# Top-k attention and a SwiGLU block: reciprocals of the first 12 units folded into the transposes on TensorE

## The chip, the cores and the metric

The kernel runs on one core of a Trainium2 chip. The metric is device time in microseconds for one launch. The engines of a core work in parallel, each through its own queue in order: TensorE (PE, with its weight loads PEld), VectorE (DVE), ScalarE (ACT), GpSimd (POOL), and SyncE (SP), which here issues nearly all DMAs. TensorE writes only into PSUM, from where ScalarE copies results into SBUF.

## The reference

Inputs q, k and v have the shape (8, 8, 576, 64): 8 batches, 8 heads, 576 positions, 64 dimensions, all fp32. The attention result becomes a matrix of 4608 rows and 512 columns, which goes through a SwiGLU block with 1536 hidden units.

```python
scores = scale * np.matmul(q, k.transpose(0, 1, 3, 2))
kth = np.partition(scores, -top_k, axis=-1)[..., -top_k:-top_k + 1]   # top_k = 32
scores = np.where(scores >= kth, scores, -1000000000.0)
scores = scores - np.max(scores, axis=-1, keepdims=True)
attn = np.exp(scores)
attn = attn / (np.sum(attn, axis=-1, keepdims=True) + 1e-09)
x = np.matmul(attn, v)            # then (B,H,S,D) -> (B*S, H*D)
g = x @ w_gate
out = (g / (1 + np.exp(-g)) * (x @ w_val)) @ w_out
```

The change concerns the division by the row sum.

## The kernel before

**Units.** The attention is cut into units: a batch, a tile of 128 query rows and a pair of heads. A batch has 576 = 4 x 128 + 64 rows, so four full query tiles and a last one of 64 rows, in which two heads share the 128 partitions. With four head pairs (`NHP` = 4) a batch has 20 units, 160 in all. The first 12 units (0 to 11) are the first three query tiles of batch 0; counted from 0, unit n is processed in iteration n of the main loop (L870), with neighbours overlapped.

**One unit, step by step.** `scores`: four products of q and k on TensorE (L325), copied and scaled by ScalarE into `sc` (L330). `select`: VectorE finds the 32 largest of each row of 576 in four rounds of MAX8 (L347) and three of MATCH_REPLACE8 (L351), for two heads. `shift`: a tiny GpSimd subtraction `bias` (L362). `weigh`: ScalarE makes the mask (L374) and the exponentials `e`, 128 x (2 x 576), with the row sums `tot` (L379), and adds the small constant (L384). `normalize`: VectorE takes the reciprocal of `tot` (L393), and for the first 12 units GpSimd multiplies each head's half of `e` by it (L399, two instructions of 128x576); from unit 12 on ScalarE does one of the two halves (L397). `turn`: TensorE transposes `e` in nine blocks of 128x128 (L412): four of head 0, one which holds the last 64 columns of head 0 and the first 64 of head 1, and four of head 1. ScalarE copies the three PSUM tiles into `et` (L413). `values`: TensorE multiplies with v (L448), ScalarE copies the result into `xT` (L465), the input of the FFN.

**The rest.** FFN work is cut into pieces that are put between the attention steps: L517 (gate and value products of the first blocks, 128 columns), L569 (first output products), L604 and L670 for all later blocks. ScalarE and GpSimd do the activation (L537 to L545, L639 to L645). The FFN weights are loaded in 36 pieces in the first 170 us and rounded by `rounded`: a DMA into a slot `w` (four slots, L109), three ScalarE instructions (L117, L119, L120), a VectorE shift (L124) and two GpSimd instructions (L125, L126). The second of these two frees the slot for the next DMA.

**Order.** The order on each engine is the order in which the program is written: at the end a dependency ties every instruction to the one before it on its engine. In iteration n the main loop issues the scores of the units ahead, `values` of units n-4 and n-3 (every second iteration), `weigh(n-1)`, the second half of the scores, the top-k of unit n with FFN pieces and weight rounding strewn in, `turn(n-2)`, then `normalize(n-1)` and `shift(n)`. So on GpSimd the bias of unit n stands behind the normalization of unit n-1. PSUM tiles of the attention come from one pool of five (`ps_t`), so `turn` also needs earlier tiles to be copied out.

Of the kernel before, what the change touches and what calls it, by code (L numbers as in the profile page):

```python
# [9 lines left out]
ALU = mybir.AluOpType  # L10
FP32 = mybir.dt.float32
# [4 lines left out]
P = 128  # L16
# [9 lines left out]
def kernel(  # L26
# [37 lines left out]
    nc = tc.nc  # L64
    B, H, S, D = q.shape
    DM, DFF = w_gate.shape
    J = S // P
    JP = J * P
    R = S - JP
    NHP = H // 2  # L70
# [4 lines left out]
    NBLK = B * S // BLK  # L75
    HALVED = 3
    AHEAD = 8 * NHP
    scale = 1.0 / float(D) ** 0.5
    assert D == 64 and R == 64 and H * D == DM and DM == 512 and B * S % BLK == 0

# [6 lines left out]
    ffn = ctx.enter_context(tc.tile_pool(name="ffn", bufs=2))  # L87
# [3 lines left out]
    ident = consts.tile([P, P], FP32, name="ident")  # L91
# [190 lines left out]
    state = {}  # L282
# [84 lines left out]
    def weigh(n):  # L367
# [10 lines left out]
        for t, hs in enumerate(heads):  # L378
# [3 lines left out]
            )  # L382
        if n < AHEAD:
            nc.scalar.add(tot[:, 0 : len(heads)], tot[:, 0 : len(heads)], EPS)  # L384
        st["tot"] = tot

    def normalize(n):
        st = state[n]
        tot, e, heads = st.pop("tot"), st["e"], st.pop("heads")
        nh = len(heads)  # L390
        for t in range(nh if n >= AHEAD else 0):
            nc.vector.tensor_scalar_add(tot[:, t : t + 1], tot[:, t : t + 1], EPS)
        nc.vector.reciprocal(tot[:, 0:nh], tot[:, 0:nh])  # L393
        yield
        for t, hs in enumerate(heads):
            if t == 0 and n >= 3 * NHP:
                nc.scalar.mul(e[:, hs], e[:, hs], tot[:, t : t + 1])  # L397
            else:
                nc.gpsimd.tensor_tensor(  # L399
                    e[:, hs], e[:, hs], tot[:, t : t + 1].to_broadcast([P, S]), ALU.mult  # L400
                )

    def turn(n):

        last = units[n][1] == J
        e = state[n].pop("e")
        et = work.tile([P, 2 * J + 1, P], FP32, tag="et", name="et")
        for c0, cn in ((0, J), (J, 1)) if last else ((0, J), (J, 1), (J + 1, J)):
            ps = ps_t.tile([P, 512], FP32, tag="t", name="etps")
            for c in range(cn):  # L410
                k0 = S - P if last and c0 == J else (c0 + c) * P
                nc.tensor.transpose(ps[:, c * P : (c + 1) * P], e[:, k0 : k0 + P], ident[:])  # L412
            nc.scalar.copy(  # L413
                et[:, c0 : c0 + cn, :],
                ps[:, 0 : cn * P].rearrange("p (c j) -> p c j", c=cn),
            )
            if c0 == J:
                yield
        state[n]["et"] = et
# [393 lines left out]
    def share(n):  # L813
# [9 lines left out]

        beside = 5.8 if n < AHEAD else 6.25
        least = 2.0 if n >= 3 * NHP and n % 2 == 0 else 0.0
# [12 lines left out]
    def pieces(n):  # L838
        for _ in range(n):
            if credit[0] >= 1:  # L840
                credit[0] -= piece()

    def run(steps):
        for _ in steps:
            pass
# [24 lines left out]
    for n in range(NU + 3):  # L870
        nh = n_heads(units[n][1]) if n < NU else 1
        topk = select(n) if n < NU else no
        norm = normalize(n - 1) if 0 <= n - 1 < NU else no
        nxt = [scores(m) for m in scored(n)]
        ahead = fetch(n + 3 if n else 2) if n + 3 < NU else no
# [42 lines left out]
        if 0 <= n - TURN < NU:  # L918
            run(turn(n - TURN))
# [6 lines left out]
        pieces(1)  # L926
        if n < AHEAD:
            run(topk)
# [55 lines left out]
```

## Time and profile before

| what | us |
|---|---|
| median of three runs | 1713.59 |
| lowest and highest | 1713.14, 1713.67 |
| the profiled execution's own time | 1712.03 |
| its span, first to last instruction | 1710.2 |
| TensorE busy in the span | 1647.4 |
| VectorE busy | 1476.5 |
| ScalarE busy | 1259.5 |
| GpSimd busy | 799.0 |

The mean granted clock of TensorE is 0.978 of full speed. A row of a timeline or of the chain of waits gives the start, the duration, the engine, and the line with the tile that it writes and those that it reads; a bracket says how long the engine was idle before it and which instruction ended that. Group rows give the number of instructions, their busy time and the mean duration of one in ns. PE instructions are pipelined, so the mean duration of one is longer than the distance from one to the next; distances are read from the chain of waits, where consecutive instructions are merged.

### The profile page before, as it was taken

Reading aid. Unit: us, or ns where it says so; the run is one execution under the profiler, and the core shown is the slowest. Engines: PE = TensorE matmul, PEld = TensorE weight load, DVE = VectorE, ACT = ScalarE, POOL = GpSimd, SP = SyncE. Lnnn points to the kernel's source line nnn. Section 1 sums busy time; section 2 is a strip of 40 time slices with the busy share of each in tenths; the row PEclk is TensorE's granted clock in tenths of the full one; section 3 lists DMA queues with packets and bytes.
Section 4 is the critical chain, followed back from the end, with each engine's and each line's share of the span. In section 5 each row is a group of like instructions: output and inputs, shape, how many; then the busy total and the mean of one; then the engine's idle time right before and its main releaser. Section 6 shows DMA issues by size and latency. Waiting matters only on the chain.

```text
span 1710.2 us, 32128 instructions
## 1 busy us (share of the span) xinstructions
PE 1647.4 (96%) x11600; PEld 1398.2 (82%) x11600; DVE 1476.5 (86%) x3311; ACT 1259.5 (74%) x2901; POOL 799.0 (47%) x914
## 2 busy tenths in 40 slices
PE   5588999999999999999999999999999999999999
PEld 3477698987888887888888888888888888888887
DVE  7999899998989899997999989998999979999400
ACT  7899887877767787768676887777777778676531
POOL 4798545352444425353535334444344433535434
PEclk6699999999999999999999999999999999999999
DMA  7533120003000030001200030000400011000000
GB/s 210 139 112 99 29 72 2 14 1 79 22 13 1 15 86 14 1 8 42 51 14 1 13 74 27 2 13 2 98 1 13 2 44 29 13 2 13 1 13 13
DMA packets 109310, 59.74 MB, mean 35 GB/s; under 512 B 88544, under 2 KB 96992, under 8 KB 109152
## 3 DMA queue, kind: packets, MB, share of 16 engines
q1 hardware_dynamic: 108016, 57.37, 12.9%
q8 instruction: 91, 1.49, 0.4%
q14 instruction: 67, 0.55, 0.1%
q10 hardware_dynamic: 1136, 0.33, 0.1%
HBM read 48.23 MB, written 9.44 MB: 34 GB/s over the span
## 4 chain that ended last, share of the span: by engine, by line
PE 88%; DVE 5%; ACT 4%; DMA 1%; POOL 1%; issue 1%; SPq 0%; POOLq 0%; ACTq 0%
PE f L604 37%; PE x_ps L670 10%; PE av L448 9%; PE s L325 8%; PE y_ps L670 8%; PE etps L412 7%; PE f L517 6%; DVE m L347 2%; DVE e L351 2%; PE kqps L271 1%; PE o_ps L569 1%; PE s L308 1%; ACT e L379 1%; DVE size L124 1%; ACT e L374 0%
## 5 line engine op out<-in xcount | busy, mean ns | idle before, releaser
L347 DVE MAX8 m<-e 128x8 f32<-128x576 f32 x864 | 617.9, 755 | 3.3
L351 DVE MATCH_REPLACE8 e<-m,e 128x576 f32<-128x576 f32 x576 | 425.4, 748 | 0.0
L604 PE MATMUL f<-xT,wg 128*128 128x256 f32 x1440 | 335.9, 382 | 1.3 <-ACT xT L465 1.3
L604 PE MATMUL f<-xT,wv 128*128 128x256 f32 x1440 | 331.4, 380 | 0.0
L604 PEld LDWEIGHTS f<-xT,wg 128*128 128x128 f32 x1440 | 268.9, 190 | 49.0 <-issue 13.1
L604 PEld LDWEIGHTS f<-xT,wv 128*128 128x128 f32 x1440 | 268.2, 190 | 37.5 <-issue 3.8
L640 POOL TENSOR_TENSOR h<-h,half_g 128x512 f32<-128x512 f32 x90 | 114.7, 1275 | 349.2 <-ACT h L639 349.2
L330 ACT ACTIVATE sc<-s 128x288 f32<-128x288 f32 x512 | 170.4, 431 | 105.2 <-PE s L325 104.6
L413 ACT COPY et<-etps 128x512 f32<-128x512 f32 (+1 forms) x448 | 183.6, 486 | 66.0 <-PE etps L412 65.6
L379 ACT ACTIVATE e<-e,bias 128x576 f32<-128x576 f32 x288 | 221.7, 780 | 12.7 <-POOL bias L362 9.7
L374 ACT ACTIVATE e<-sc,m 128x576 f32<-128x576 f32 x288 | 212.3, 792 | 0.6 <-DVE m L347 0.5
L351 DVE MATCH_REPLACE8 e<-m,sc 128x576 f32<-128x576 f32 x288 | 212.6, 748 | 0.0
L412 PE MATMUL etps<-ident,e 128*128 128x128 f32 x1312 | 178.2, 280 | 33.7 <-POOL e L399 15.0
L347 DVE MAX8 m<-sc 128x8 f32<-128x576 f32 x288 | 204.0, 747 | 7.5 <-ACT sc L330 7.5
L412 PEld LDWEIGHTS etps<-ident,e 128*128 128x128 f32 x1312 | 156.2, 144 | 54.7 <-POOL e L399 19.2
L645 POOL TENSOR_TENSOR h<-h,val 128x512 f32<-128x512 f32 x90 | 114.8, 1275 | 155.0 <-ACT val L644 152.4
L325 PE MATMUL s<-kqT 64*128 64x288 f32 x1024 | 169.2, 441 | 13.7 <-ACT sc L330 7.5
L399 POOL TENSOR_TENSOR e<-e,tot 128x576 f32<-128x576 f32 x140 | 161.1, 1154 | 28.5 <-DVE tot L393 28.2
L448 PE MATMUL av<-et,v 128*64 128x128 f32 (+1 forms) x2560 | 158.0, 268 | 0.0
L448 PEld LDWEIGHTS av<-et,v 128*64 128x64 f32 x2560 | 137.7, 140 | 5.9 <-ACT kqT L268 2.7
L325 PEld LDWEIGHTS s<-kqT 64*128 64x128 f32 x1024 | 94.2, 190 | 58.3 <-issue 18.4
L397 ACT ACTIVATE e<-e,tot 128x576 f32<-128x576 f32 x148 | 119.1, 805 | 21.7 <-DVE tot L393 21.6
(86 smaller groups left out, 2249.1 us busy)
## 6 DMA issues: line engine op xcount, KB each, us to landing
v<-in_v_dram SPq DMA_DIRECT2D x32, 256.0 KB, 3.3
kq_in<-in_k_dram SPq DMA_DIRECT2D x63, 128.0 KB, 2.8
kq_in<-in_q_dram SPq DMA_DIRECT2D x63, 128.0 KB, 2.9
w<-in_moe_w_gate_dram SPq DMA_DIRECT2D x12, 512.0 KB, 3.8
w<-in_moe_w_val_dram SPq DMA_DIRECT2D x12, 512.0 KB, 3.8
w<-in_moe_w_out_dram SPq DMA_DIRECT2D x12, 512.0 KB, 3.5
out_dram<-o SPq DMA_DIRECT2D x38, 128.0 KB, 2.4
out_dram<-o SPq DMA_DIRECT2D x16, 256.0 KB, 2.5
```

What stands on the lines that cost most here:

```text
L325: nc.tensor.matmul(ps[:, 0:half], slab[d, q0 : q0 + P], slab[d, k0 : k0 + half])
L330: nc.scalar.mul(sc[:, i * half : (i + 1) * half], ps[:, 0:half], scale)
L347: nc.vector.max(m[:, t, 8 * r : 8 * r + 8], cur[:, hs])
L351: nc.vector.match_replace(e[:, hs], m[:, t, 8 * r : 8 * r + 8], cur[:, from_[t]], LOWEST)
L374: nc.scalar.activation(e[:, hs], sc[:, at], AF.Prelu, bias=m[:, t, TOP_K - 1 : TOP_K], scale=-1.0, alpha=SMALL,)
L379: nc.scalar.activation(e[:, hs], e[:, hs], AF.Exp, bias=bias[:, t : t + 1], scale=-1.0 / SMALL, accum_out=tot[:, t : t + 1],)
L399: nc.gpsimd.tensor_tensor(e[:, hs], e[:, hs], tot[:, t : t + 1].to_broadcast([P, S]), ALU.mult)
L412: nc.tensor.transpose(ps[:, c * P : (c + 1) * P], e[:, k0 : k0 + P], ident[:])
L413: nc.scalar.copy(et[:, c0 : c0 + cn, :], ps[:, 0 : cn * P].rearrange("p (c j) -> p c j", c=cn),)
L448: nc.tensor.matmul(av[d, i, 0:ql], weights_, moving, start=c == (0 if last else J), stop=c == (J if last else J - 1),)
L604: nc.tensor.matmul(ps[:, i, :], w[:, kc, m * P : (m + 1) * P], x[:, kc, :], start=(kc == 0), stop=(kc == KC - 1),)
L670: nc.tensor.matmul(ps, lhsT, T[i][m], start=m == 0, stop=m == MQ - 1)
```

## The change

For units 0 to 11 (`SCALED = 3 * NHP`), `e` stays as the exponentials left it. GpSimd instead builds two 128x128 diagonal matrices, one for each head, with the reciprocals on the diagonal (one instruction of 128x256, from the identity matrix and `tot`). `turn` then multiplies with a diagonal matrix in place of the transpose: `e` block as the stationary operand, the diagonal matrix as the moving one, which transposes and scales at once. The block that holds columns of both heads is split into two products of 64 columns each, since its halves need different reciprocals. Four pairs of diagonal matrices are kept, in a buffer that has the tag of the FFN's output tile `o`. Units from 12 on are as before.

```diff
+    SCALED = 3 * NHP
...
+    scaling = []
+
     def normalize(n):
...
         nc.vector.reciprocal(tot[:, 0:nh], tot[:, 0:nh])
         yield
+        if n < SCALED:
+            if not scaling:
+                scaling.append(ffn.tile([P, 4, 2, P], FP32, tag="o", name="diag", bufs=1))
+            st["diag"] = diag = scaling[0][:, n % 4]
+            nc.gpsimd.tensor_tensor(
+                diag,
+                ident[:].unsqueeze(1).to_broadcast([P, 2, P]),
+                tot[:].unsqueeze(2).to_broadcast([P, 2, P]),
+                ALU.mult,
+            )
+            return
...
+        diag = state[n].pop("diag", None)
...
-                nc.tensor.transpose(ps[:, c * P : (c + 1) * P], e[:, k0 : k0 + P], ident[:])
+                at = slice(c * P, (c + 1) * P)
+                if n >= SCALED:
+                    nc.tensor.transpose(ps[:, at], e[:, k0 : k0 + P], ident[:])
+                elif c0 == J:
+                    for t in range(2):
+                        d = slice(t * R, (t + 1) * R)
+                        nc.tensor.matmul(
+                            ps[d, at],
+                            e[:, k0 + t * R : k0 + (t + 1) * R],
+                            diag[:, t],
+                            start=True,
+                            stop=True,
+                        )
+                else:
+                    nc.tensor.matmul(
+                        ps[:, at], e[:, k0 : k0 + P], diag[:, c0 // J], start=True, stop=True
+                    )
```

## The prediction

> **What bounds the kernel now.** I read the page from the top: busy shares, then the forty slices.
>
> ```profile
> PE 1647.4 (96%) x11600; PEld 1398.2 (82%) x11600; DVE 1476.5 (86%) x3311; ACT 1259.5 (74%) x2901; POOL 799.0 (47%) x914
> ...
> PE   5588999999999999999999999999999999999999
> DVE  7999899998989899997999989998999979999400
> ACT  7899887877767787768676887777777778676531
> POOL 4798545352444425353535334444344433535434
> PEclk6699999999999999999999999999999999999999
> ```
>
> From the fifth slice (171 us) on TensorE is full at full clock; before that it has gaps and a low clock. The twelve units that change lie there: the last of their GpSimd multiplications ends at 167.7 us. The same cut by stretches:
>
> ```profile
> 0.00:168.40 168.40, 117.86 (x845) 98.22 (x846) 155.61 (x323) 147.09 (x326) 127.97 (x122) 0.79 0.51 142
> 168.40:400.00 231.60, 228.02 (x1961) 194.93 (x1961) 213.67 (x464) 181.39 (x434) 111.65 (x126) 1.00 0.10 25
> ```
>
> The columns are span, then PE, PEld, DVE, ACT, POOL busy, granted clock, DMA. After 168.4 us PE lacks only 3.6 of 231.6 us, so the end moves by as much as the moment moves when PE gets there. Before it PE idles 50 us; there the question is what sets the pace. The chain of waits, asked for 100 to 180 us, answers it:
>
> ```profile
> 105.71 2.48 POOL e L399 x2
> 108.19 0.34 POOL bias L362
> ...
> 112.44 1.30 POOL wg L126
> 113.76 3.54 DMA w<-in_moe_w_out_dram
> 117.39 0.68 ACT size L117
> ...
> 132.54 0.27 ACT xT L465
> 132.94 2.15 PE etps L412 x9
> 135.10 7.04 PE f L517 x48
> ```
>
> GpSimd, with a multiplication in its queue, frees a weight slot late; the DMA behind it lands late; ScalarE then runs back to back up to the xT copy, which gives unit 8's transposes their PSUM slot. From there PE is without a gap, but for one place, in PE's timeline:
>
> ```profile
> 160.32 1.15 PE L412 MATMUL etps<-ident,e 128*128 128x128 f32 x9
> ...
> 166.65 0.66 PE L412 MATMUL etps<-ident,e 128*128 128x128 f32 x4 [1.61 <-POOL e L399]
> 167.76 0.76 PE L412 MATMUL etps<-ident,e 128*128 128x128 f32 x5 [0.45 <-POOL e L399]
> ```
>
> These are units 10 and 11; unit 11 waits 2.06 us for its two multiplications. The rows that price the operations are groups kept apart by shape:
>
> ```profile
> L412 PE MATMUL etps<-ident,e 128*128 128x128 f32 x1312 | 178.2, 280 | 33.7 <-POOL e L399 15.0 <-ACT xT L465 12.5 <-ACT e L397 3.5
> L448 PE MATMUL av<-et,v 128*64 128x128 f32 x2048 | 136.8, 277 | 0.0
> L690 POOL TENSOR_TENSOR xT<-h 128x256 f32<-128x256 f32 x51 | 36.8, 731 | 27.7 <-PE x_ps L670 25.5
> ```
>
> **What is removed on GpSimd.** Two 128x576 multiplications per unit took 2.25 to 2.48 us together (24 instructions, median 1152 ns). **Added:** one 128x256 multiplication. Its nearest row is L690's, 731 ns for 128x256; the bounds are 0.19 (bias, 128x2) and 1.15 us (128x576). I take 0.73, so GpSimd gains 1.5 to 1.75 us per unit, about 19 us in twelve. Little of it is on the path. Three places pay:
> - At 82.5 us ScalarE waits 0.73 us for the bias, queued directly behind unit 4's multiplications. The bias comes about 1.5 us earlier, so this wait goes; the xT copy behind it and the first FFN product start 0.73 earlier.
> - At 117.39 ScalarE waits 1.01 us for w_out. Two multiplications stand before that slot's release in the continuous GpSimd run from 89.8 us, so it frees some 3 us earlier and the wait goes. What is late next is ScalarE itself, without a gap to 138 us.
> - Unit 11's 2.06 us. Its diagonal matrix is still queued behind L545, L125 and L126, and starts at about 165.3, ready at 166.0.
>
> VectorE's weight shifts (L124) take 403 ns at best, 704 in the median, 1492 at most, and the long ones end when a GpSimd instruction ends; five that lie over a multiplication lose 3.5 us (excesses 0.61, 0.66, 0.60, 0.94, 0.67). I cost this at nothing: between 104 and 148 us the chain runs through GpSimd, ScalarE and PE. If ScalarE had slack, this would be the next gain.
>
> **What is added on TensorE.** Line 448 issues 1280 products with v in the program text (8 per unit, 160 units); the rows show 2048 + 512 = 2560. Line 412 issues 1312 transposes and shows 1312. So an fp32 product is two PE instructions, a transpose one. A unit goes from 9 instructions to 2 x 8 full and 2 x 2 of 64 columns. In the chain nine transposes at full clock take 0.98 us (0.109 each), 48 product instructions with 128 columns 5.36 (0.112 each), 40 of av with 64 weight columns 2.33 (0.058, two side by side). After: 16 x 0.112 + 4 x 0.058 = 2.02, and some 0.06 for two changes of array shape, so +1.1 us per unit. The bounds are +1.04 and, if the halves do not run side by side, 20 x 0.112 - 0.98 = +1.26. At half clock the nine take 2.15, the new ones 16 x 0.239 + 4 x 0.117 = 4.29: +2.14.
>
> The Trainium skill ("TensorE: Matmul & The Clock Gate", Terms) calls transpose mode four times faster for FP32. By that a unit would cost 3 x 0.98 = +2.9 us at full clock instead of +1.1, and the sum below would end some 5.4 us higher; the rows here show 0.109 against 2 x 0.112, a factor of two, and I go by them.
>
> Units 0 to 7 transpose where PE idles 2 to 5 us on either side. I cost them at nothing; the cover is PE's wait for ScalarE before each, and if a copy of et (ScalarE, in order) has to wait for the last product, it costs up to 0.9 us (unit 6: products would end at about 115.0, its third copy stood at 114.1).
>
> **The new waits.** The diagonal matrices use the buffer of the first output tile; ScalarE first writes that at 189.5 us, 20 us after unit 11. The fifth matrix waits for PE's unit 0, four units back. L124 gets a wait on GpSimd in the program, on an older piece that its ScalarE producer already awaited. All three cost nothing.
>
> **The sum on the path,** from the xT copy at 132.5 on:
> - unit 8's start: -0.73 - 1.01 = -1.74;
> - unit 8's products at half clock: +2.14;
> - the clock: it rose at 49.7, 80.4, 114.6, 121.4 and 138.5 us and fell at 118.0 and 131.7, all multiples of about 3.4 us apart, and a rise needs such a slice nearly full. If PE starts at 131.2 instead of 132.94, the slice from 131.7 is full and the rise comes 3.4 us earlier, worth 1.7 us. That hangs on a phase no one sets: -0.85, bounds 0 and -1.7;
> - units 9 and 10 in the gapless stretch: 2 x 1.1 = +2.2;
> - unit 11: +1.1 - 2.06 = -0.96. PE arrives at about 166.8, after the matrix.
>
> Together +0.79 us. The profiled execution took 1712.03 us (span 1710.2), so it would take 1712.8; the median of the three others is 1.56 above it, and on that median the forecast is 1714.4.
>
> The skill (same page, PE-mode transpose) holds that transposes do not count as activity for the clock; by it, products in their place would bring the early rise for certain, a sum of about -0.1. The rise at 49.7 followed a slice with 2.4 us of transposes in it, so the trace does not bear that out.
>
> **Rivals.**
> - *TensorE's low clock takes the gain back: slower.* Longer transposes of unit 3 fill the slice 70 to 73.5, the clock rises early, the products after it finish at 79 instead of 82, PE idles 5 us and the first FFN product at 84 starts at half clock: +1.55. Unit 6 then holds up ScalarE by 0.9. The start of unit 8 is +0.71 instead of -1.74, the clock term 0: 0.71 + 2.14 + 2.2 - 0.96 = +4.1, 1717.7 us. It decides once ScalarE loses over 1.74 us between 84 and 117. For it: PEclk 0.5 for 60 to 80 us. Against: ScalarE's copies mostly have 1 to 2 us of slack.
> - *GpSimd's relief reaches further: faster.* ScalarE also loses four waits for weights before 80 us (0.76, 0.86, 0.99, 0.84 = 3.45), and the clock rises early: -1.74 - 3.45 + 2.14 - 1.7 + 2.2 - 0.96 = -3.5, 1710.1 us. Against: those slots are freed by pieces that waited for VectorE, not for a multiplication.
> - *The products cost no more than transposes.* Then -1.74 - 0.85 - 2.06 = -4.65, 1708.9 us. The doubled record counts speak against it.
>
> **How the numbers follow.** Forecast 0.70, slower rival 0.18, far relief 0.09, cheap products 0.03. A measurement here tells 0.2% (3.4 us) from no change, so same is 1710.2 to 1717.0. Two thirds of the slower rival and a tail of the forecast lie above (0.14), two thirds of the two fast ones below, with a little of the forecast (0.08); 0.78 remains. The range from 1711.5 to 1718.0 holds the forecast with its bounds (-0.2 to +2) and most of the slower rival.
>
> **What would show it.** GpSimd's busy time before 168 us falls by about 19 us; about 240 PE instructions read the diagonal matrices, the transposing of units 9 and 10 grows from 1.0 to about 2.1 us each; no wait of unit 11 for GpSimd; L117's wait at 117 gone; PE without a gap from 131 to 134 us on. A shift of the gapless stretch beyond 3 us either way would make me wrong, above all through ScalarE's order before 117 us or through the clock.

## The result and the profile after

| | before | after |
|---|---|---|
| median, us (22 runs each; the three shown before are among them) | 1713.29 | 1715.92 |
| lowest and highest | 1711.63, 1714.59 | 1714.77, 1718.19 |
| own time of the profiled execution | 1712.03 | 1715.13 |
| its span | 1710.2 | 1713.3 |

The ratio is 1.0018, with an interval from 1.0012 to 1.0024: the changed kernel is 0.18% slower (0.15%, 2.6 us, by the medians alone; 3.1 us by the two profiled executions). The forecast was +0.8 us. The sign that it gave is right, and the time lies in its range, but three quarters of the loss were not in its sum.

Line numbers below are those of the changed kernel: L402 builds the diagonal matrices, L441 and L433 are the products that transpose (whole blocks, and blocks of 64 columns), L444 the copy of et, L496 that of xT, L548 the FFN products, L568 to L571 their activation, L118 to L121 ScalarE's part of a weight piece. L429 are the transposes and L413 the multiplications of `e` in the units that keep them, L352 is VectorE's MATCH_REPLACE8, L396 its reciprocal. In the versions with more lines they shift by two.

The page of the changed kernel, busy times and three rows of the forty slices:

```profile
PE 1664.1 (97%) x11732; PEld 1413.5 (82%) x11732; DVE 1475.0 (86%) x3311; ACT 1259.0 (73%) x2901; POOL 778.3 (45%) x902
...
PE   6698999999999999999999999999999999999999
...
POOL 4677544343444424353535334444344443535434
PEclk6699999999999999999999999999999999999999
```

TensorE has 132 instructions and 16.7 us more, GpSimd 12 instructions and 20.7 us less. From the fifth slice on TensorE is full at full clock, as it was. Up to 168.4 us, with the columns span, PE, PEld, DVE, ACT, POOL, granted clock, DMA share, GB/s:

```profile
0.00:168.40 168.40, 131.42 (x949) 110.64 (x950) 150.34 (x316) 144.36 (x322) 106.97 (x109) 0.79 0.49 139
```

GpSimd falls from 127.97 to 106.97 us here, TensorE rises from 117.86 to 131.42. The groups kept apart by shape, for the start of the changed kernel (count, then busy time and mean ns of one):

```profile
L402 POOL TENSOR_TENSOR diag<-ident,tot 128x256 f32<-128x256 f32 x12 | 7.7, 643 | 0.1
L441 PE MATMUL etps<-diag,e 128*128 128x128 f32 x192 | 37.1, 354 | 15.7 <-ACT xT L496 10.3 <-POOL diag L402 5.4
L433 PE MATMUL etps<-diag,e 128*64 128x128 f32 x48 | 6.8, 372 | 1.6 <-ACT sc L331 1.6
```

So 240 product instructions stand where 108 transposes stood. Now the order of events. TensorE's timeline around the first FFN product, before and after:

```profile
84.71 3.39 PE L517 MATMUL f<-xT,wg 128*128 128x128 f32 x28 [2.52 <-ACT xT L465]
```

```profile
78.64 0.71 PE L548 MATMUL f<-xT,wg 128*128 128x128 f32 x4
83.75 4.88 PE L548 MATMUL f<-xT,wg 128*128 128x128 f32 x28 [4.40 <-ACT xT L496]
```

and its stretches (span, PE busy, then PEld, DVE, ACT, POOL, granted clock), two of the kernel before and four of the changed one:

```profile
77.00:80.50 3.50, 3.50 (x34) 3.17 (x32) 3.50 (x9) 2.66 (x7) 3.42 (x4) 0.51 0.75 243
80.50:84.00 3.50, 1.70 (x12) 1.02 (x11) 3.50 (x10) 2.77 (x6) 2.01 (x3) 1.00 0.63 167
```

```profile
73.50:77.00 3.50, 2.99 (x42) 2.33 (x40) 3.50 (x8) 3.47 (x10) 3.42 (x3) 1.00 0.30 57
77.00:80.50 3.50, 2.35 (x22) 1.54 (x18) 3.50 (x8) 2.75 (x7) 3.42 (x4) 1.00 0.74 232
80.50:84.00 3.50, 0.25 (x1) 0.26 (x2) 3.50 (x8) 3.47 (x10) 0.22 (x2) 0.93 0.59 163
84.00:87.40 3.40, 3.40 (x19) 3.40 (x20) 3.40 (x10) 0.91 (x4) 2.66 (x2) 0.57 0.00 0
```

The clock is full from about 73 us (before: from 80.4), the products behind unit 3's transposing are over by 79.4, TensorE has nothing to do for 4.40 us, and the 28 product instructions that follow get a clock of 0.57 and take 4.88 us; before they took 3.39. ScalarE needs that result. What ScalarE waited for between 84 and 134 us (total, times, longest), before and after:

```profile
ACT h L537 <- PE f L517: 2.3, 1, 2.3
ACT size L117 <- DMA w<-in_moe_w_out_dram: 1.0, 1, 1.0
```

```profile
ACT h L568 <- PE f L548: 3.8, 1, 3.8
ACT et L444 <- PE etps L441: 1.3, 1, 1.3
```

The wait for the FFN product has grown by 1.5 us, the one for w_out is gone, and unit 6's third copy now waits for the longer products. The fall of the clock at that product is not the changed kernel's alone. Of the profiles with no filling ahead of it (the experiments below included), the three with products in the units before all show it: 4.88, 5.90 and 5.50 us for the 28 instructions, after a rise between 73 and 75 us. Of four with transposes, where the clock rose between 78.5 and 80.4 us, three took 3.36 to 3.39 us and one, of a kernel that up to there is the kernel before, 5.02. So an execution of the kernel before can pay this too, and the +1.49 us below holds for the two executions compared.

The chain of waits of the changed kernel shows both waits, and what follows:

```profile
83.43 0.27 ACT xT L496
...
83.75 4.89 PE f L548 x28
...
88.66 0.60 ACT h L568
...
111.32 2.05 PE etps L441 x8
113.37 0.63 PE etps L433 x4
113.99 2.02 PE etps L441 x8
...
133.77 2.05 PE etps L441 x8
135.82 0.62 PE etps L433 x4
136.44 1.90 PE etps L441 x8
138.34 8.93 PE f L548 x80
147.28 0.89 PE etps L441 x8
148.17 0.37 PE etps L433 x4
148.54 1.09 PE etps L441 x8
```

Where before GpSimd and a DMA stood in the chain between 104 and 117 us, there are now ScalarE and TensorE alone. Unit 8 starts at 133.77 instead of 132.94, and at half clock its twenty instructions take 4.57 us; units 9 to 11 take 2.35 us each (0.89 + 0.37 + 1.09) where 0.98 stood. Unit 11 waits for nothing.

### The profile page after: what moved, and what is told of

Same layout as the page of the kernel before. It is cut to its first block, busy times and chain, and to the rows that moved or that the text cites. A ratio compares the mean times of both kernels' runs of the same rounds, so it can differ in the third digit from the quotient of the medians.

```text
span 1713.3 us, 32373 instructions
## 1 busy us (share of the span) xinstructions
PE 1664.1 (97%) x11732; PEld 1413.5 (82%) x11732; DVE 1475.0 (86%) x3311; ACT 1259.0 (73%) x2901; POOL 778.3 (45%) x902
## 4 chain that ended last, share of the span: by engine, by line
PE 89%; ACT 5%; DVE 3%; DMA 1%; issue 1%; SPq 0%; POOL 0%; ACTq 0%; POOLq 0%
PE f L635 36%; PE x_ps L701 10%; PE av L479 9%; PE s L326 8%; PE y_ps L701 8%; PE etps L429 7%; PE f L548 7%; DVE e L352 1%; PE kqps L272 1%; DVE m L348 1%; PE o_ps L600 1%; ACT e L380 1%; PE s L309 1%; PE etps L441 1%; ACT et L444 1%
## 5 line engine op out<-in xcount | busy, mean ns | idle before, releaser
L352 DVE MATCH_REPLACE8 e<-m,e 128x576 f32<-128x576 f32 x576 | 423.8, 742 | 0.0
L444 ACT COPY et<-etps 128x512 f32<-128x512 f32 (+1 forms) x448 | 183.9, 486 | 70.3 <-PE etps L429 67.0
L352 DVE MATCH_REPLACE8 e<-m,sc 128x576 f32<-128x576 f32 x288 | 211.9, 742 | 0.0
L429 PE MATMUL etps<-ident,e 128*128 128x128 f32 x1204 | 156.3, 273 | 4.3 <-ACT e L411 3.5
L429 PEld LDWEIGHTS etps<-ident,e 128*128 128x128 f32 x1204 | 140.0, 141 | 19.7 <-ACT e L411 4.0
L413 POOL TENSOR_TENSOR e<-e,tot 128x576 f32<-128x576 f32 x116 | 133.0, 1147 | 29.7 <-DVE tot L396 29.5
```

Source lines behind the costliest of these rows:

```text
L352: nc.vector.match_replace(e[:, hs], m[:, t, 8 * r : 8 * r + 8], cur[:, from_[t]], LOWEST)
L413: nc.gpsimd.tensor_tensor(e[:, hs], e[:, hs], tot[:, t : t + 1].to_broadcast([P, S]), ALU.mult)
L429: nc.tensor.transpose(ps[:, at], e[:, k0 : k0 + P], ident[:])
L444: nc.scalar.copy(et[:, c0 : c0 + cn, :], ps[:, 0 : cn * P].rearrange("p (c j) -> p c j", c=cn),)
```

## The experiments

Two theories are held against each other. **Theory B:** TensorE's longer transposing and its low clock delay ScalarE between 84 and 117 us, and that takes GpSimd's 1.74 us of relief and more. **Theory A:** the loss is product time in TensorE's gapless stretch, from unit 8 on; TensorE's work ahead of unit 8 costs the end nothing, as the forecast had it. Unit 8's late start must then come from a gain of GpSimd's that did not reach ScalarE. Each run is compared with runs of the kernel before beside it, and each ratio below is against that.

### Products alone, and relief alone

The first kernel keeps GpSimd's multiplications of `e` and transposes by products with the identity matrix:

```diff
-        if n < SCALED:
+        if n < 0:
...
-                            diag[:, t],
+                            ident[:],
...
-                        ps[:, at], e[:, k0 : k0 + P], diag[:, c0 // J], start=True, stop=True
+                        ps[:, at], e[:, k0 : k0 + P], ident[:], start=True, stop=True
```

> Units 0 to 11 transpose by products with the identity matrix, split as in the change, and GpSimd multiplies e as before: TensorE's part of the change alone. Theory A (the loss is product time in TensorE's gapless stretch): units 9 and 10 cost 1.36 us each, unit 11 1.36 less the 2.06 us that it waited before, unit 8 some 0.8: +2.8 us against the kernel before. Theory B (the loss is TensorE's low clock, which reaches the path through ScalarE): besides these the first FFN product at 84 us runs at half clock (+1.5 us) and unit 6 holds ScalarE up by 1.3 us, of which 1.0 is absorbed by the wait for a weight slot at 117 us: +4.6 us.

Measured: 1718.21 us, ratio 1.0025 (1.0016 to 1.0034), +4.6 us. That is theory B's number, but the lower end of the interval, +2.7 us, reaches theory A's +2.8; the trace has to decide. Its chain of waits:

```profile
85.48 5.90 PE f L548 x28
...
116.25 1.99 PE etps L441 x8
118.25 0.04 DVEq L352
118.28 0.04 issue
118.32 1.55 DVE e L352 x3
...
136.33 2.05 PE etps L441 x8
```

The first FFN product is slower still (5.90 us, after 5.20 us without work on TensorE), and unit 8 starts 3.39 us later than before. On the way unit 6's products release a buffer of `e` at 118.25 for which VectorE has waited. So TensorE's part alone delays unit 8's start, by an amount that theory A has no place for. (Without filling or change ahead of unit 8, its start also moves between executions: 132.94 and, in the run with unit 11 alone below, 133.47 us. That is far less than 3.39.)

The second kernel builds the diagonal matrices but transposes with the identity matrix. It leaves out the division by the row sum in units 0 to 11.

```diff
-                if n >= SCALED:
+                if n >= 0:
```

> GpSimd builds the diagonal matrices in place of its two multiplications, and TensorE transposes with the identity as before, so the division is left out for units 0 to 11: GpSimd's part of the change alone. Both theories: unit 11's wait goes (-2.06 us). If ScalarE's two waits (0.73 and 1.01 us) go as well and are carried to unit 8, -4 us, with a clock that rises one step earlier -5.7 us. If the relief reaches no further than unit 11, -2 us.

Measured: 1707.80 us, ratio 0.9966 (0.9954 to 0.9979), -5.9 us. Its chain at unit 8:

```profile
130.51 2.18 PE etps L429 x9
132.69 5.71 PE f L548 x48
```

Unit 8 starts 2.43 us earlier than before, so GpSimd's gain does reach ScalarE, with more than the 1.74 us forecast. Theory A has no way out left. The two parts add up at that place: 3.39 - 2.43 = +0.96, against +0.83 in the changed kernel. Put the other way, TensorE's part costs 3.39 us at unit 8's start without the relief and 3.26 with it (133.77 against 130.51). The two parts don't add up at the end (4.6 - 5.9 = -1.3 against +2.6). Of that difference 2.06 us is unit 11's wait, which each of them removes: one because TensorE comes later, one because GpSimd is done earlier.

### Which units

Products in units 0 to 8 only, the three units in the gapless stretch as before:

```diff
-    SCALED = 3 * NHP
+    SCALED = 9
```

> The change for units 0 to 8 only. Theory A: without 1.36 us each for units 9 and 10, and with unit 11 back to a transpose and part of its wait, 2.7 us below the changed kernel, so about +0.4 us against the kernel before (unit 8's +1.7 less the remaining relief of unit 11). Theory B: the shift of unit 8 by +1.7 us at the end of its FFN product stays in full, and a shorter wait of unit 11 takes back at most 1 to 1.5: about +0.5 us. This run does not tell A from B, it prices units 9 to 11.

Measured: 1716.56 us, ratio 1.0014 (1.0005 to 1.0023), +2.9 us: a miss. Sparing units 9 to 11 the products brought nothing. The chain of waits:

```profile
144.38 0.60 ACT h L568
...
150.80 0.17 DVE tot L396
...
167.89 0.10 POOL e L413
...
168.81 1.15 POOL e L413
...
170.01 1.31 PE etps L429 x5
171.32 2.88 PE f L548 x16
```

The path to unit 11 does not run through TensorE here. It leaves at the FFN product behind unit 8, for which ScalarE's `h` waits (144.38, before 142.16), and goes over the reciprocal on VectorE (150.80, before 148.59) to GpSimd's multiplication (167.89, before 165.63). All of it is 2.2 us late, TensorE waits for it again, and the clock falls in that wait: 1.31 and 2.88 us for what took 0.76 and 1.79. A unit's products in the gapless stretch are a cost only where TensorE gets there last.

Unit 11 alone:

```diff
-        if n < SCALED:
+        if n == 11:
...
-                if n >= SCALED:
+                if n != 11:
```

> Only unit 11 gets its diagonal matrix and products, all others as before. Both theories: nothing moves before 165 us; unit 11 costs 1.36 us more and its wait of 2.06 us shrinks to what the matrix takes: -0.7 us against the kernel before, a version that would beat both.

Measured: 1712.68 us, ratio 0.9994 (0.9986 to 1.0003): not told from no change. The wait of 2.06 us became one of 1.11 us for the diagonal matrix, which stands behind the same weight pieces on GpSimd.

### Holding the clock up

If the half clock is the cause, work without any use in the idle stretch must give the time back. In the changed kernel 38 transposes of the identity matrix into an unused PSUM tile go ahead of the rest of the first FFN product:

```diff
+    FILL_A = 38
+    FILL_T = {}
...
+                    if (kb, t, g, i, kc) == (0, 0, 0, 0, 1) and w is wg:
+                        fill(FILL_A)
...
+    def fill(k):
+        if k:
+            idle = ps_f.tile([P, P], FP32, tag="f", name="idle")
+        for _ in range(k):
+            nc.tensor.transpose(idle[:], ident[:], ident[:])
...
+            fill(FILL_T.get(n - TURN, 0))
             run(turn(n - TURN))
```

> The changed kernel with 38 transposes of the identity into an unused PSUM tile in TensorE's gap before the rest of the first FFN product (79.4 to 83.8 us), so that its clock stays up there. Theory B (low clock through ScalarE): that product takes 3.4 us instead of 4.9, ScalarE goes on 1.5 us earlier at 88 us, and if unit 6 holds it up no more than now, unit 8 starts 1.5 us earlier: -1.5 us against the changed kernel, up to -3 with a clock that rises one step earlier at unit 8. Theory A (product time in the gapless stretch): no change.

Measured: 1713.87 us, ratio 1.0000 (0.9991 to 1.0009). Added work made the changed kernel faster, by some 2 us by the medians and 1.3 us by the profiled executions; theory A has 0. TensorE's timeline:

```profile
79.40 4.31 PE L882 MATMUL idle<-ident 128*128 128x128 f32 x38
83.99 3.39 PE L550 MATMUL f<-xT,wg 128*128 128x128 f32 x28 [0.28 <-ACT xT L498]
```

The same 28 instructions take 3.39 us, and unit 8 starts at 132.53, 1.24 us earlier than in the changed kernel.

Next the same, with 22 transposes ahead of unit 6 and 36 ahead of unit 8:

```diff
-    FILL_T = {}
+    FILL_T = {6: 22, 8: 36}
```

> As the one before, and 22 such transposes before unit 6 and 36 before unit 8, in the gaps of 2.6 and 4.3 us there. Theory B: unit 6 transposes in 2.35 us and no longer holds ScalarE up (1.33 us less), unit 8 in 2.35 instead of 4.41: together with the first product -1.5 - 1.3 - 2.1 = -4.9 us against the changed kernel, below the kernel before. Theory A: only unit 8's 2.1 us.

Measured: 1709.13 us, ratio 0.9976 (0.9966 to 0.9986): 4.4 us faster than the kernel before. Its stretches and its chain at unit 8:

```profile
80.50:84.00 3.50, 3.02 (x27) 2.78 (x26) 3.50 (x8) 3.47 (x10) 0.20 (x2) 1.00 0.48 154
84.00:87.40 3.40, 3.40 (x32) 3.40 (x32) 3.40 (x10) 1.13 (x5) 2.66 (x2) 1.00 0.02 5
```

```profile
131.00 1.13 PE etps L443 x8
132.13 0.37 PE etps L435 x4
132.50 1.09 PE etps L443 x8
133.59 8.93 PE f L550 x80
```

Unit 8 starts 2.77 us earlier than in the changed kernel and its twenty instructions take 2.59 us instead of 4.57. ScalarE has no wait for unit 6's products any more. Against the version with the first filling alone unit 8 starts 1.53 us earlier, so both of the terms that theory B names, 1.49 and 1.33 us, come back when the clock is held up.

### How much of that is the filling itself

The kernel before, with 34 transposes ahead of unit 8 only, and then with 22, 34 and 36 at the three places:

> The kernel before with 34 such transposes in the gap of 3.9 us before unit 8. There unit 8's transposes took 1.95 us instead of 0.98 at full clock and the FFN product behind them 3.42 instead of 1.79: -2.6 us against the kernel before if the clock is what costs there, 0 if PE's place in line is set by something else.

Measured: 1712.77 us, ratio 0.9996 (0.9987 to 1.0004), not the -2.6 us expected. In its profiled execution the filling did its work: from unit 8's transposes to unit 9's it is 9.91 us, against 12.59 in the kernel before. But the first FFN product had fallen to half clock (5.02 us at 84.63), and unit 8 started 1.23 us late. Unit 11 then waited as before, for a multiplication to which the chain of waits leads through VectorE and GpSimd from before 128 us on, not through unit 8. In that wait the clock fell, and the 16 FFN instructions behind it took 3.11 us instead of 1.78. The first output products start at 170.08 us, before at 170.14.

> The kernel before with transposes of the identity in its gaps before the rest of the first FFN product (22), unit 6 (34) and unit 8 (36): the clock is held up, GpSimd and the transposes are as before. If the gain of the same filling in the changed kernel came from the clock alone, it is had here as well: about -2.8 us at unit 8, and 1.5 in executions in which the first product falls to half clock; -2.8 to -4 us against the kernel before, level with the changed and filled kernel. If the relief of GpSimd is what the full clock lets through, this one gains -1 to -2 at most, as the unit 8 filling alone did, since unit 11 still waits for GpSimd and ScalarE for its weight slot.

Measured: 1710.85 us, ratio 0.9988 (0.9979 to 0.9997), -2.1 us. What TensorE waited for between 60 and 175 us, first line:

```profile
PE etps L414 <- POOL e L401: 11.5, 6, 4.4
```

In the changed kernel with fillings at the same three places, waits for GpSimd are down to one of 1.7 us, for a diagonal matrix. Even so the change adds little here. The fillings alone give 2 us of the 4.4, and the two profiled executions show where the rest lies. The first output products start at 168.26 us in this one and at 168.58 us with the change, so up to there the change has gained nothing beside the fillings. From there to the end of the span the times are 1540.0 and 1538.6 us: here the clock falls once more near the end (0.50 from 1642 to 1645 us), in the other it does not. The next section takes up that fall.

### A version that is faster than both

As the version with three fillings, but units 9 and 10 keep their transposes and GpSimd's multiplications:

```diff
-    SCALED = 3 * NHP
+    SCALED = (*range(9), 11)
...
-        if n < SCALED:
+        if n in SCALED:
...
-                if n >= SCALED:
+                if n not in SCALED:
```

> The changed kernel with the three fillings, and the change for units 0 to 8 and 11 only: units 9 and 10 in the gapless stretch are transposed and multiplied by GpSimd as before. Theory of product time: 2 x 1.36 = -2.7 us against the changed and filled kernel (about -7 against the kernel before) if GpSimd, with its work for units 9 and 10 back, has unit 11's matrix ready before TensorE arrives; if not, the wait eats up to 1.1 us of it, as in the run with unit 11 alone.

Measured: 1709.12 us, ratio 0.9979 (0.9970 to 0.9988), the same as with all twelve units, though its first output products start at 167.15 us against 168.58. Unit 11 again waits 1.13 us for its diagonal matrix, behind the multiplications of units 9 and 10. And the 1.4 us that are left went at the far end: TensorE idles 1.78 us ahead of unit 159's transposes, at 1638 to 1641 us, and in this profile the clock then fell, in that of the version with all twelve units not. From the first output products to the end it is 1540.2 us with the fall and 1538.6 without. The kernel before and the changed kernel have the same idle stretch and the same fall, with 1540.1 and 1540.0 us. From 1640 to 1647 us (span, PE busy, granted clock, DMA share, GB/s):

```profile
1640.00:1647.00 7.00, 6.92 (x61) 0.76 0.26 60
```

Whether holding the clock up there brings the difference out was tried with 15 transposes more at that place, in both versions:

```diff
-    FILL_T = {6: 22, 8: 36}
+    FILL_T = {6: 22, 8: 36, 159: 15}
```

> The changed kernel with the three fillings, and 15 identity transposes (1.64 us) ahead of unit 159's transposes, where TensorE idles 1.78 us at about 1640 us. Theory C: whether the clock falls after that idle stretch is a matter of the phase of its slices, and a fall costs about 1.5 us; the profiled execution of the version without this filling had no fall and took 1708.97, its executions lie in two groups, 1708.74 to 1709.14 (five) and 1710.35 to 1710.62 (three). Then only the lower group is left: median about 1709.0, highest under 1709.5, no half clock after 1641 us. Rival D: the two groups come from the first 170 us; then both groups stay, the filling makes no difference beyond 0.2 us.

Measured, all twelve units: 1709.05 us, ratio 0.9975 (0.9964 to 0.9985). The median stays within 0.1 us, as expected, but the upper group is not gone altogether: seven executions lie between 1708.27 and 1709.30, one at 1710.20.

> Units 0 to 8 and 11 changed, with the three fillings, and the same 15 transposes ahead of unit 159's. Theory C: the profiled execution of the version without it had half clock from 1641 to 1644.6 us and took 1709.12, with the time at which the first output products start 1.4 us earlier than in the version with all twelve units; its executions reach from 1707.31 to 1710.51. Without the fall the median is about 1707.6, 1.4 below the version with all twelve. Rival D: the median stays at 1709.1 and the spread at 3.2 us.

Measured, units 0 to 8 and 11: 1708.29 us (1707.60 to 1708.84), ratio 0.9969 (0.9958 to 0.9980). The spread falls from 3.2 to 1.2 us and the median by 0.8, not by the 1.5 expected. Its row of the same stretch:

```profile
1640.00:1647.00 7.00, 6.94 (x68) 1.00 0.25 58
```

So the fall at the end goes with most of the spread in one version and, with one execution out of eight, not all of it in the other. The gain of 0.8 us is not told from none by the ratios, whose intervals overlap. This version has the lowest median of those that keep the division, 0.31% below the kernel before. How much of that is the change and how much the four fillings stays open, since the kernel before was not run with all four. By one execution each, the first output products start at 167.12 us here and at 168.26 us in the kernel before with three fillings, a gain of 1.1 us.

## Why the prediction was right or wrong

The terms of its sum, as the two profiles have them:

| step | forecast, us | measured, us |
|---|---|---|
| bias earlier, first FFN product's start (84.71 to 83.75) | -0.73 | -0.96 |
| first FFN product at half clock | not in the sum | +1.49 |
| wait for w_out at 117 | -1.01 | -1.01 |
| unit 6's third copy of et waits | 0 (up to 0.9 named) | +1.33 |
| unit 8's start, these together | -1.74 | +0.83 |
| unit 8's products | +2.14 | +2.46 |
| clock rise, on the FFN product behind | -0.85 (0 to -1.7) | -1.63 |
| units 9 and 10 | +2.2 | +2.73 |
| unit 11 | -0.96 | -1.13 |
| sum | +0.79 | +3.26 |

TensorE's first output products start at 173.33 instead of 170.14 us (+3.19), and the span is 3.1 us longer, so the measured terms hold the whole of the difference between these two executions. Unit 8's products and the clock's rise are read from TensorE's timeline: 4.41 against 1.95 us to the start of the next product, and 1.79 against 3.42 us for that product. The clock's term came out near its bound by luck: the forecast let unit 8 start earlier, so that the clock would rise 3.4 us earlier. Unit 8 started later, and the clock rose at about 138.1 instead of 138.5 us; the longer products took up the time at half clock, and the FFN product behind them came after the rise.

**The step that failed** is "Units 0 to 7 transpose where PE idles 2 to 5 us on either side. I cost them at nothing". The cover that was named, TensorE's wait for ScalarE, hides the length of the transposing but not two things that come out of it. The longer work of unit 3 moves the clock's rise from 80.4 to about 73 us (78.5 to 80.4 in the five profiles with transposes there, 72 to 75 in the eight with products), so the work behind it ends earlier, the idle stretch grows to 4.40 us and the next product starts at a low clock; ScalarE waits for that product. And unit 6's last product, at half clock, is later than ScalarE's copy: "up to 0.9 us" was 1.33. Both were written down in the rival that ends slower, with unit 8's start at +0.71; it was +0.83. The condition that the rival set, a loss of ScalarE above 1.74 us between 84 and 117, came true: 1.49 + 1.33 = 2.82. The runs show the cause twice over. TensorE's part moves unit 8's start by 3.39 us alone and by 3.26 on top of the relief; and with the idle stretches filled unit 8 starts 2.77 us earlier than in the changed kernel, 1.24 of it from the first filling. By the medians the three fillings bring the changed kernel from 2.6 us behind the kernel before to 4.4 ahead of it. Not all of this is damage of the change undone: the kernel before gains 2.1 us by fillings too, and the fall near the end, which no filling of the three touches, makes 1.5 us between the profiled executions. A chance of 0.18 for that rival was too little, given that its chain of events was worked out and nothing stood against it but that the copies "mostly have 1 to 2 us of slack".

**The rival's own sum** of +4.1 was too high in one term and too low in others: it took the clock's rise at 0, while the longer products of unit 8 filled the slice by themselves and the FFN product behind took 1.79 us instead of 3.42.

**GpSimd's gain** was priced nearly right in busy time: the wait for w_out is gone, busy time fell by 21.0 us (forecast 19), and a diagonal matrix took 0.61 us in the median (0.73 taken, between 0.19 and 1.15). Its reach was priced low: alone it brings unit 8 forward by 2.43 us, not 1.74. The far-reaching rival, -3.5, is not what happened in the changed kernel; with the relief alone it was -5.9, of which 2.06 is unit 11's wait.

**The products** cost 2.35 us per unit at full clock, +1.37 instead of +1.1 and above the upper bound of +1.26. The halves of the split block do run side by side, as the forecast took it: in the trace the two products of a pair start 0.007 us apart, as av's do. The term that was mis-sized is the change of array shape, 0.06 us in the forecast. At full clock the first half starts 0.205 us behind the last whole block, the next whole block 0.203 us behind the last half, and the one after that 0.213 us later, where consecutive products of whole blocks are 0.112 us apart. In all it is 2.35 - 16 x 0.112 - 4 x 0.058 = 0.33 us a unit. The rival in which products cost no more than transposes fell with the first row.

**Unit 11** came out nearly as forecast. But its wait of 2.06 us belongs to a path over ScalarE, VectorE and GpSimd: in the three runs with units 9 and 10 back on GpSimd it came back, with 1.1 to 2.1 us.

**Two rules that the prediction weighed.** The products that replace nine transposes took 2.35 us against 0.98, a factor of 2.4 with the split block and its changes of shape; going by the rows was right. The Trainium skill ("TensorE: Matmul & The Clock Gate", Terms) calls transpose mode four times faster for FP32, without saying than what; against products no run here shows that. As to the clock, 38 transposes and nothing else, from 79 to 83 us, kept the granted clock at 1.00 where it had fallen to 0.57 without them. In the run with the relief alone transposes also brought it up: from 61.6 to 65.0 us TensorE ran nothing else, was busy for 2.94 of 3.40 us at a clock of 0.50, and got 1.00 from 65.0 us on. The same page, PE-mode transpose, holds that transposes do not count as activity for the clock. The measurement decides against the rule.

**What was not tried:** VectorE has a new wait, 4.2 us in three places, for products to release a buffer of `e`, which the prediction did not list. In the kernel with the products alone it lies on the chain of waits, in the changed kernel it does not between 83 and 173 us. No run had another buffer of `e`, so its price stays open.

## What to carry to other kernels

Work that is moved onto an engine with idle time is free only if neither its last instruction nor the clock that it changes reaches anyone: ask who waits for the next result of that engine, and at what clock that result will be made. Before a saving on one engine is added up, take the next path that leads to the same instruction, as with unit 11, where TensorE, and GpSimd by way of VectorE and ScalarE, arrive about 2 us apart. Where idle stretches of 2 to 5 us lie ahead of work on the path, idle transposes that hold TensorE's clock can be worth more than the change itself: here they gave 2.1 us in the kernel before, where the change by itself cost 2.6.

## What the runs showed of the hardware

- Work that ran earlier can make what follows slower: with full clock from 73 us on, TensorE ran dry for 4.40 us and the next 28 instructions took 4.88 instead of 3.39 us; with 38 idle transposes in the gap 3.39 again.
- TensorE's clock counted transposes here: 38 of them held it at 1.00 from 79 us on, and a stretch of 3.4 us with transposes alone (2.94 us busy) was followed by a rise from 0.50 to 1.00.
- An idle stretch of 1.78 us in TensorE near the end (1638 to 1641 us) was followed by a granted clock of 0.76 over 7 us in the profiled execution of one version; in that of another the clock stayed at 1.00. From the first output products on, eight profiles with the fall took 1540.0 to 1540.2 us and the three without it 1538.6 to 1538.7, so a fall costs about 1.5 us. (Two more with the fall took 1541.3 and 1541.7; the second of these shows another fall at 396 us.) What decides whether it comes no run shows.
- Twelve multiplications of 128x256 with two broadcast inputs took 0.61 us in the median, less than the 0.73 us of plain ones of that size.
- Two products with 64 weight columns into the two halves of the output's partitions start 0.007 us apart. Changing from 128 to 64 weight columns and back costs about 0.33 us at full clock, the same in every unit that ran at full clock.
